# Summing k and v in four column tiles, and the gate on VectorE

## The chip, the cores and the metric

One core of a Trainium2 chip runs the kernel. The metric is the device time of one execution in microseconds, as the median of several runs. PE (TensorE) multiplies and writes PSUM, DVE (VectorE) and ACT (ScalarE) work element by element, POOL (GpSimd) does a little of that and issues some DMAs, and SP (SyncE) only issues DMAs. Each engine takes its instructions in the order in which they are written; a semaphore wait holds all that stands behind it on that engine.

## The reference

Two branches read the same x (2048 rows of 512) and are mixed row by row by a gate. Branch a is attention with 32 heads of 16 columns that share one k and one v; branch b is a dense layer with a squared relu.

```python
g = sigmoid((x * gate_w).sum(-1))
q = x @ wq            # 32 heads x 16
k, v = x @ wk, x @ wv # 16 columns each, shared by all heads
a = softmax(q k^T * 16 ** -0.5) v, heads side by side, @ wo
b = relu(x @ w1 + b1) ** 2 @ w2 + b2      # 1792 hidden columns
out = g * a + (1 - g) * b
```

All of it is in float32. The kernel forms products of large operands in pieces: each operand is rounded to a value `r` that TensorE takes at its fast rate and a rest `l`, and three products (rr, rl, lr) are added.

## The kernel before

The program is unrolled and written in the order in which the engines are to work. It has an opening, a long sequence of phases, and an end.

**The opening (lines 246 to 596).** x comes in transposed, in four chunks of 512 rows with four 128-row pieces each (`xf`, `xk`). A matrix `wkv` of 64 columns holds wk, wv, gate_w and 31 columns of zeros, so that one product gives k, v and the gate's argument. `kv_half` (L290) does it in two column tiles of 64: pieces 0 and 1 go to partitions 0 to 63 and 64 to 127 of one PSUM bank, then pieces 2 and 3 are added there. `kv_copy` (L299) brings the bank to SBUF on ScalarE. `k_rows` (L302) adds up the two halves and repeats the keys for the heads with one more product; ScalarE squares (`k_square`) and rounds them (`k_round`), `k_norm` (L315) sums the squares on TensorE and takes their maximum on VectorE, `k_parts` builds `k_aug`. The maximum over all four chunks gives a bound that `k_shift` (L324) writes into a row of `k_aug`; scores need it. `v_tiles` (L332) turns v, and the gate's argument as a seventeenth column, into rows, with one product for each 128 rows; with `idle=1` a product of 240 columns whose result nobody reads follows each. `v_rows` copies v to `v_ext` and the gate's argument to `z`. Nine of the sixteen tiles come ahead of the first phase with their idle products, seven behind it without (L1210). `q_early` makes the first q, `q_direct` and `qnorm` send it to the first score operand `qa`.

**The phases (lines 1134 to 1234).** Each phase writes scores for a few blocks (L763, into `s` banks that ScalarE turns into exponentials at L800, or into the one spare bank `x`, from which VectorE copies them at L784 first), mixes them with products of a "unit" (L1107), and ends with the context products over earlier exponentials (L814; four column tiles of 32, eight records for each 512 columns of four heads). Units are first fifteen q products, then hidden units of the dense layer (`hidden`, L651) and their sums. When a unit is through, its bank is evicted on VectorE at the end of a phase (for a q unit L392 to L396, for a hidden unit L662, L663 and `split`, L192 and L193). A second bank takes the next unit; the one after needs the evicted one.

**What orders the rest.** A planner in the Python code keeps clocks for TensorE, VectorE and ScalarE (`at_pe`, `at_dve`, `at_act`). `spend` (L621) fits small tasks on VectorE into what it takes for free time: first `soon`, with fixed due times, then `divisions`, then `chores` in their order. A chore that starts a load returns the time for which the following chores are held back (`LANDS`, 6 us, for the load of wo at L942). `soon` holds, among others, the gate (L517: two exponentials of `z` on ScalarE, four small steps on VectorE), due in the fourteenth span.

**DMAs.** Nearly all loads and the writes of q (`qs`) stand in SP's queue in written order; the low part of q goes through POOL. Ten tiles named "of" serve q's parts, norms and the hidden parts by turns.

Of the kernel before, what the change touches and what calls it, by code (L numbers as in the profile page):

```python
# [57 lines left out]

C_ID, C_BLK, C_A, C_ONE, C_SEL, C_REP, C_N = 0, 128, 160, 161, 162, 179, 307


def constants():
    c = np.zeros((128, C_N), np.float32)
    c[:, :128] = np.eye(128)
    for p in range(128):
        c[p, C_BLK + p // 32 * 2 + p % 2] = 1.0
    for r in range(2):
        c[64 * r + 16:64 * r + 32, C_A] = -1.0
    c[:, C_ONE] = 1.0
    for a in (0, 64):  # L70
        for d in range(17):
# [91 lines left out]
@with_exitstack  # L163
def mix_kernel(ctx: ExitStack, tc: tile.TileContext, xT, wkv, wq, wo, w12, b1, b2, cst, out):
    nc = tc.nc
# [62 lines left out]
    with fast, tc.tile_pool(name="at", bufs=1) as at, \  # L228
# [42 lines left out]
        wq_load(slice(1, KT))  # L271
        nc.gpsimd.dma_start(b1t, b1)

        blk = at.tile([128, 32], BF, name="blk")
# [9 lines left out]
        kvp = [sp.tile([128, 2, CH], F32, name="s") for _ in range(2)]  # L284
        ks = {0: kvp[0][:, 0], 1: kvp[0][:, 1], 3: kvp[1][:, 0]}
        sqk = at.tile([96, NC, CH], BF, name="sqk", tag="e", bufs=5)
        kvc = at.tile([128, NC, CH], F32, name="kvc", tag="e", bufs=5)
        kvq, kb = {}, {}

        def kv_half(c, a):  # L290

            if a == 0:
                kvq[c] = mp.tile([128, CH], F32, name="mm")
            for i in range(2):
                k = 2 * a + i
                nc.tensor.matmul(kvq[c][64 * i:64 * i + 64], wkvf[:, k], xf[c, k], start=a == 0, stop=a == 1,  # L296
                                 skip_group_check=True, tile_position=(0, 64 * i))

        def kv_copy(c):  # L299
            nc.scalar.activation(kvc[:, c], kvq[c], AF.Copy)  # L300
# [14 lines left out]
        def k_norm(c):  # L315
            pn = kvp[0][:, 0] if c > 1 else mp.tile([128, CH], F32, name="mm")
            nc.tensor.matmul(pn, ones, sqk[:, c], start=True, stop=True)
            return lambda: nc.vector.tensor_reduce(kmx[:, c:c + 1], pn, AX.X, OP.max)
# [13 lines left out]
        def v_tiles(tiles, vp, idle=0):  # L332

            for i in tiles:
                c, j = divmod(i, 4)
                nc.tensor.matmul(vp[:, i * 17:i * 17 + 17], kvc[:, c, j * 128:(j + 1) * 128],
                                 cs[:, C_SEL:C_SEL + 17], start=True, stop=True)
                for _ in range(idle):
                    nc.tensor.matmul(vp[:, 272:], ones, sqk[:, 0, 272:], start=True, stop=True)

        def v_rows(vp):
            vz = vp[:, :16 * 17].rearrange("p (i d) -> p i d", i=16)
            nc.vector.tensor_copy(v_ext[:, :, 0:32:2], vz[:, :, :DH])
            nc.vector.tensor_copy(z, vz[:, :, DH])

# [189 lines left out]

        qa[0] = at.tile([128, 2, CH], F32R, name="qa", bufs=2)
        kv_half(0, 0)
        x_pair(0, 0)
        kv_half(0, 1)
        kv_copy(0)  # L540
        x_pair(0, 1)
        nc.vector.tensor_copy(blk, cs[:, C_BLK:C_BLK + 32])
        qr, ql, q_round, q_rest = q_early()
        k_rows(0)
        x_pair(1, 0)
        q_round()
# [3 lines left out]
        q_direct(RS + 1, ql, DH, (nc.sync, nc.gpsimd))  # L550
        kv_half(1, 0)
        kv_half(1, 1)
        k_square(0)
        k_round(0)
        norm = k_norm(0)
        x_pair(1, 1)
        norm()
        kv_copy(1)
        kv_half(2, 0)
        kv_half(2, 1)  # L560
        k_rows(1)
        kv_copy(2)
        qnorm([(0, sq8[:, 0])], bank())
        k_square(1)
        k_round(1)
        k_parts(0)
        kv_half(3, 0)
        kv_half(3, 1)
        k_parts(1)
        kv_copy(3)  # L570
        wq_round(1)
        wq_rest(1)
        k_rows(2)
        norm = k_norm(1)
        norm()
        k_square(2)
        k_round(2)
        k_rows(3)
        norm = k_norm(2)
        norm()  # L580
        k_square(3)
        vp = ap.tile([128, CH], F32, name="acc")
        v_tiles(range(3), vp, 1)
        norm = k_norm(3)
# [6 lines left out]
        k_shift(0, True)  # L591
        v_tiles(range(3, 9), vp, 1)
        k_parts(3)
# [11 lines left out]
        soon += [(6, 1.2, lambda k=k: x_split(2, k)) for k in range(KT)]  # L605
        soon += [(10, 1.2, lambda k=k: x_split(3, k)) for k in range(KT)] + [(14, 2.0, gate)]
        ring, h, b2t, x, osp = [], [], [], dict(enumerate(zip(xr, xl))), {}

        def later(f, *args):
            chores.append((1.2, lambda: f(*args)))  # L610

        def have(half, n):
# [324 lines left out]
        def o_ready(c):  # L937

            if c == 0 and not wos:
                wos.extend(xp.tile(sh, F32R, name=n, tag=t) for n, t in (("wor", "xr2"), ("wol", "xl2")))  # L940

                def load(a):  # L942
                    nc.sync.dma_start(stage()[:, :2], wo[a * 256:a * 256 + 256].rearrange("(t p) n -> p t n", p=128))
# [75 lines left out]
        def work():  # L1019
# [3 lines left out]
            def places(unit):  # L1023
# [3 lines left out]
                def ready(p):  # L1027
                    assert not narrow
                    big = xp.tile(sh, F32, name="big", tag="xr3")
# [179 lines left out]
        evicted = True  # L1209
        v_tiles(range(9, 16), vp)  # L1210
        v_rows(vp)
# [74 lines left out]
```

## Time and profile before

| | us |
|---|---|
| median of 3 runs | 1226.75 (1225.81 to 1229.14) |
| the profiled execution | 1228.71 |
| its span | 1227.0 |
| ScalarE busy in it | 1035.5 |
| VectorE busy in it | 771.2 |

A busy TensorE at 99% says little by itself, since its matmuls overlap and their ends are modelled. What helps is a table of stretches, with TensorE's busy time and the clock that it was granted, and the timeline where one of the two is low. A step from one context group (L814) to the next serves as a yardstick, because the phases are alike: a group of 16 records closes a phase with four score blocks, a group of 24 one with six.

### The profile page before, as it was taken

Reading aid. Unit: us, or ns where it says so; the run is one execution under the profiler, and the core shown is the slowest. Engines: PE = TensorE matmul, PEld = TensorE weight load, DVE = VectorE, ACT = ScalarE, POOL = GpSimd, SP = SyncE. Lnnn points to the kernel's source line nnn. Section 1 sums busy time; section 2 is a strip of 40 time slices with the busy share of each in tenths; the row PEclk is TensorE's granted clock in tenths of the full one; section 3 lists DMA queues with packets and bytes.
Section 4 is the critical chain, followed back from the end, with each engine's and each line's share of the span. In section 5 each row is a group of like instructions: output and inputs, shape, how many; then the busy total and the mean of one; then the engine's idle time right before and its main releaser. Section 6 shows DMA issues by size and latency. Waiting matters only on the chain.

```text
span 1227.0 us, 24104 instructions
## 1 busy us (share of the span) xinstructions
PE 1211.2 (99%) x9839; PEld 673.4 (55%) x9839; DVE 771.2 (63%) x1516; ACT 1035.5 (84%) x1146; POOL 66.3 (5%) x87
## 2 busy tenths in 40 slices
PE   9999989999999999999999999999999999999997
PEld 4555545555555555555555555555555555555553
DVE  5765768466576864837678574655848476663643
ACT  6788868888988888888888888988888888988875
POOL 1001020000000200000002001000010000001000
PEclk9999989999999999999999999999999999999999
DMA  6344331121113223112133122112132222113011
GB/s 227 78 120 117 102 88 49 48 75 40 52 57 120 88 74 91 53 32 66 57 100 117 57 61 92 49 40 74 38 91 64 57 67 81 36 31 91 23 52 37
DMA packets 45347, 88.71 MB, mean 72 GB/s; under 512 B 10642, under 2 KB 10898, under 8 KB 44720
## 3 DMA queue, kind: packets, MB, share of 16 engines
q1 hardware_dynamic: 37024, 68.27, 18.7%
q0 software_dynamic: 8064, 18.59, 4.9%
q8 instruction: 79, 1.29, 0.5%
q14 instruction: 36, 0.29, 0.1%
q10 hardware_dynamic: 144, 0.26, 0.1%
HBM read 57.83 MB, written 20.97 MB: 64 GB/s over the span
## 4 chain that ended last, share of the span: by engine, by line
PE 93%; DVE 2%; ACT 2%; DMA 1%; SPq 1%; issue 1%; DVEq 0%; ACTq 0%
PE acc L814 37%; PE mm L1107 33%; PE s L763 17%; PE x L763 6%; ACT e L800 1%; DVE e L784 1%; SPq L420 1%; DMA stage<-in_wo 0%; DMA xf<-in_xT 0%; PE mm L296 0%; PE mm L200 0%; DVE qr L392 0%; DVE ql L393 0%; PE s L306 0%; DVE ot L1249 0%
## 5 line engine op out<-in xcount | busy, mean ns | idle before, releaser
L800 ACT ACTIVATE e<-s 128x1024 f32<-128x1024 f32 x822 | 781.7, 1026 | 165.9 <-PE s L763 165.3
L784 DVE COPY e<-x 128x512 f32<-128x512 f32 x404 | 279.1, 691 | 389.1 <-PE x L763 354.1
L814 PE MATMUL acc<-e,v_ext 128*32 128x512 f32 (+1 forms) x4224 | 484.3, 586 | 0.0
L763 PE MATMUL s<-qa,k_aug 49*128 49x512 f32 x1644 | 462.4, 413 | 0.2
L763 PEld LDWEIGHTS s<-qa,k_aug 49*128 49x128 f32 x1644 | 234.8, 185 | 75.0 <-ACT e L800 54.0
L814 PEld LDWEIGHTS acc<-e,v_ext 128*32 128x32 f32 x4224 | 116.1, 109 | 241.9 <-issue 238.2
L1107 PE MATMUL mm<-w2r,hr 64*128 64x512 f32 x896 | 229.2, 402 | 0.0
L800 ACT ACTIVATE e<-e 128x1024 f32<-128x1024 f32 x202 | 214.7, 1063 | 0.8 <-DVE e L784 0.8
L763 PE MATMUL x<-qa,k_aug 49*128 49x512 f32 x404 | 164.7, 408 | 5.4 <-DVE e L784 4.2
L1107 PEld LDWEIGHTS mm<-w2r,hr 64*128 64x128 f32 x896 | 135.7, 186 | 45.9 <-DVE hr L193 9.2
L1107 PE MATMUL mm<-w2l,hr 64*128 64x512 f32 x448 | 143.9, 392 | 0.0
L763 PEld LDWEIGHTS x<-qa,k_aug 49*128 49x128 f32 x404 | 75.1, 186 | 51.3 <-DVE w2l L491 12.6
L1107 PEld LDWEIGHTS mm<-w2l,hr 64*128 64x128 f32 x448 | 80.5, 186 | 6.9
L1107 PE MATMUL mm<-xragain,w1r 64*128 64x512 f32 x224 | 76.3, 418 | 0.2
L1107 PE MATMUL mm<-xr,w1r 64*128 64x512 f32 x224 | 74.3, 416 | 0.0
L1107 PE MATMUL mm<-xlagain,w1r 64*128 64x512 f32 x224 | 74.0, 391 | 0.0
L1107 PE MATMUL mm<-xragain,w1l 64*128 64x512 f32 x224 | 73.1, 392 | 0.0
L1107 PE MATMUL mm<-xl,w1r 64*128 64x512 f32 x224 | 72.4, 391 | 0.0
L1107 PE MATMUL mm<-xr,w1l 64*128 64x512 f32 x224 | 72.0, 395 | 0.0
L839 DVE RECIPROCAL n<-n 128x86 f32<-128x86 f32 x90 | 61.5, 683 | 1.8
L1107 PEld LDWEIGHTS mm<-xragain,w1r 64*128 64x128 f32 x224 | 38.2, 185 | 27.7 <-issue 9.2
L1107 PEld LDWEIGHTS mm<-xr,w1r 64*128 64x128 f32 x224 | 37.9, 185 | 26.8 <-issue 8.4
(162 smaller groups left out, 1181.4 us busy)
## 6 DMA issues: line engine op xcount, KB each, us to landing
stage<-in_w SPq DMA_DIRECT2D x56, 256.0 KB
qa<-qs SPq DMA_DIRECT2D x186, 64.0 KB
w1f<-in_w SPq DMA_DIRECT2D x28, 256.0 KB
w2f<-in_w SPq DMA_DIRECT2D x28, 256.0 KB
qs<-qr SPq DMA_DIRECT2D x16, 256.0 KB
ress<-res POOLq DMA_DIRECT2D x4, 1024.0 KB, 5.1
qs<-ql POOLq DMA_DIRECT2D x15, 256.0 KB, 7.5
oc<-accs SPq DMA_DIRECT2D x30, 128.0 KB
```

The costliest lines, as they stand in the source:

```text
L420: nc.sync.dma_start(bass.AP(tensor=o.tensor, offset=o.offset, ap=[[KS * 2 * CH, 4], [CH, 2], [1, CH]]), nrm[32 * i:32 * i + 8].bitcast(F32))
L763: nc.tensor.matmul(dst.rearrange("p (a n) -> p a n", a=2), k_aug[rows, kt * 128:(kt + 1) * 128], qa[it][rows, :, q * HC:q * HC + HC], star ...
L784: nc.vector.tensor_copy(e_half(u)[:, 2 * r:2 * r + 2], x.rearrange("p (a n) -> p a n", a=2))
L800: nc.scalar.activation(e_half(u), src, AF.Exp, scale=SCALE)
L814: nc.tensor.matmul(acc[h * 32:(h + 1) * 32, cols], v_ext[:, kt], es[u // 2][:, h % 2 * 2 + h // 2, mine], start=(kt == 0), stop=(kt == NK ...
L839: return ((0.23, bound), (0.35, compare), (0.72, lambda: nc.vector.reciprocal(n[0], n[0])), (0.28, lambda: nc.vector.tensor_tensor(o[:, co ...
L1107: nc.tensor.matmul((self.before if r else self).bank, a[p], b[p], start=not r and i == 0, stop=r == 1 and i == len(self.terms[1]) - 1, ski ...
```

## The change

- `wkv` has 32 columns (wk and wv), and `kv_sums` does the four pieces of a chunk as four column tiles of 32 at once, each in its own 32 partitions of the bank. `k_rows` and `v_tiles` add up four strips instead of two by the constant matrices. The weights' load moves from the head of SP's queue to ScalarE's. The bank is "mm" for even chunks and the spare bank "x" for odd ones.
- The gate's argument is no longer a column of that product. Sixteen blocks of 128 rows of x, not transposed, and gate_w broadcast to all partitions are loaded by SP in four groups (`gate_load`), into "of" tiles; VectorE multiplies each with gate_w and sums along the row in one instruction (`gate_sum`, L621 of the changed kernel). These are chores ahead of all others, each group held for 10 us. The gate itself is a chore behind them, and `gated` makes sure of it when the first hidden unit is evicted.
- The load of wo holds its chores back for 14 us (`WRITES`) instead of 6.
- The opening is written in another order, norms share one half of the second `s` tile, and 12 v tiles stand ahead of the first phase, 4 behind it, all with idle products.

```diff
-LANDS, DIVIDES, SURE = 6.0, 10.0, 0.7
+LANDS, DIVIDES, WRITES, SURE = 6.0, 10.0, 14.0, 0.7
...
-        wkvf = at.tile([128, KT, 64], F32, name="wkvf", tag="w1f")
-        nc.sync.dma_start(wkvf, wkv)
+        wkvf = at.tile([128, KT, 32], F32, name="wkvf", tag="w1f")
+        nc.scalar.dma_start(wkvf, wkv)
...
-            for i in range(2):
-                k = 2 * a + i
-                nc.tensor.matmul(kvq[c][64 * i:64 * i + 64], wkvf[:, k], xf[c, k], start=a == 0, stop=a == 1,
-                                 skip_group_check=True, tile_position=(0, 64 * i))
+            for k in parts:
+                nc.tensor.matmul(kvq[c][32 * k:32 * k + 32], wkvf[:, k], xf[c, k], start=True, stop=True,
+                                 skip_group_check=True, tile_position=(0, 32 * k))
...
-            pn = kvp[0][:, 0] if c > 1 else mp.tile([128, CH], F32, name="mm")
+            pn = kvp[0][:, c % 2] if c in (1, 2) else norms
...
-            nc.vector.tensor_copy(z, vz[:, :, DH])
...
-        soon += [(10, 1.2, lambda k=k: x_split(3, k)) for k in range(KT)] + [(14, 2.0, gate)]
+        soon += [(10, 1.2, lambda k=k: x_split(3, k)) for k in range(KT)]
...
+        def gate_load(i):
+            if i == 0:
+                nc.sync.dma_start(gwb, bass.AP(tensor=gw.tensor, offset=gw.offset, ap=[[0, 128], [1, D]]))
+            gates.extend(of_tile("xs", F32) for _ in range(4))
+            for j in range(i, i + 4):
+                nc.sync.dma_start(gates[j], xs[j])
+            return DIVIDES
+
+        def gate_sum(i):
+            nc.vector.scalar_tensor_tensor(gates[i], gates[i], 1.0, gwb, op0=OP.mult, op1=OP.mult,
+                                           accum_out=z[:, i:i + 1])
+
+        for i in range(NS):
+            if i % 4 == 0:
+                chores.append((0.0, lambda i=i: gate_load(i)))
+            chores.append((0.7, lambda i=i: gate_sum(i)))
+        chores.append((2.0, gate))
...
-                    return LANDS
+                    return WRITES
...
-        v_tiles(range(9, 16), vp)
+        v_tiles(range(12, 16), vp, 1)
```

Three places show how the instructions move. First TensorE in the opening, from the first sums of k and v (`mm` or `x` from `wkvf`) to the last chunk's; `cs` holds the constant matrix of `k_rows`, `ones` and `blk` are the norms' weights. Before:

```order
L296 MATMUL mm<-xf,wkvf 64x512 x4
L200 MATMUL mm<-xf,wqf 128x512 x4
L306 MATMUL s<-kvc,cs 128x512
L296 MATMUL mm<-xf,wkvf 64x512 x4
L317 LDWEIGHTS ones
L317 MATMUL mm<-sqk,ones 128x512
L296 MATMUL mm<-xk,wkvf 64x512 x4
L306 MATMUL s<-kvc,cs 128x512
L413 LDWEIGHTS blk
L413 MATMUL mm<-sq_142,blk 32x512
L296 MATMUL mm<-xk,wkvf 64x512 x4
```

Now:

```order
L297 MATMUL mm<-xf,wkvf 32x512 x4
L200 MATMUL mm<-xf,wqf 128x512 x4
L297 MATMUL x<-xf,wkvf 32x512 x4
L307 MATMUL s<-kvc,cs 128x512
L297 MATMUL mm<-xk,wkvf 32x512 x4
L307 MATMUL s<-kvc,cs 128x512
L412 LDWEIGHTS blk
L412 MATMUL s<-sq_143,blk 32x512
L318 LDWEIGHTS ones
L318 MATMUL s<-sqk,ones 128x512
L307 MATMUL mm<-kvc,cs 128x512
L297 MATMUL x<-xk,wkvf 32x512 x4
```

The second chunk's sums stand ahead of the first key rows, the first norm of the keys moved behind the q norm, and both norms are now in the same half tile.

Second, VectorE around the first two evictions of hidden units (`big` from `mm` with b1, then the square and the two parts); `wor` and `wol` are the parts of wo. Before:

```order
L784 COPY e<-x 128x2x256 x2
L662 TENSOR_SCALAR big<-mm,b1t 128x512
L663 TENSOR_TENSOR big<-big 128x512
L192 CAST hr<-big 128x512
L193 TENSOR_TENSOR hr<-big,hr 128x512
L784 COPY e<-x 128x2x256
L491 TENSOR_TENSOR w1l<-stage,w1r 128x512
L784 COPY e<-x 128x2x256
L192 CAST wor<-stage 128x512
L193 TENSOR_TENSOR wol<-stage,wor 128x512
L784 COPY e_1883<-x 128x2x256
```

Now:

```order
L806 COPY e<-x 128x2x256 x2
L519 TENSOR_SCALAR g<-g 128x16
L520 RECIPROCAL g<-g 128x16
L519 TENSOR_SCALAR omg<-omg 128x16
L520 RECIPROCAL omg<-omg 128x16
L684 TENSOR_SCALAR big<-mm,b1t 128x512
L685 TENSOR_TENSOR big<-big 128x512
L192 CAST hr<-big 128x512
L193 TENSOR_TENSOR hr<-big,hr 128x512
L806 COPY e<-x 128x2x256
L490 TENSOR_TENSOR w1l<-stage,w1r 128x512
L806 COPY e<-x 128x2x256
```

The gate, which stood 100 rows further up, is now ahead of the first eviction, and the splits of wo are gone from here: the first now follows the second hidden unit and one more w1 split.

Third, SP's queue at the same place, from the norm writes on. Before:

```order
L420 DMA qs<-nrm 4x2x512 x4
L943 DMA stage<-in_wo 128x2x512
L1033 DMA big<-in_b 128x512
L474 DMA stage<-in_w 128x512
L943 DMA stage<-in_wo 128x2x512
L474 DMA w1f<-in_w 128x512
```

Now:

```order
L419 DMA qs<-nrm 4x2x512 x4
L1056 DMA big<-in_b 128x512
L965 DMA stage<-in_wo 128x2x512
L473 DMA stage<-in_w 128x512
L473 DMA w1f<-in_w 128x512
L204 DMA oc<-accs 64x512
```

The load of b2 changes places with the first load of wo, and the second load of wo moves behind the next load of q.

More of the change, by code (lines that the diff above doesn't have):

```diff
@@ L69, in constants @@
     c[:, C_ONE] = 1.0
-    for a in (0, 64):
-        for d in range(17):
+    for a in range(0, 128, 32):
+        for d in range(DH):
             c[a + 16 + d, C_SEL + d] = 1.0
@@ L163, in mix_kernel @@
 @with_exitstack
-def mix_kernel(ctx: ExitStack, tc: tile.TileContext, xT, wkv, wq, wo, w12, b1, b2, cst, out):
+def mix_kernel(ctx: ExitStack, tc: tile.TileContext, xT, xs, gw, wkv, wq, wo, w12, b1, b2, cst, out):
     nc = tc.nc
@@ L272, in mix_kernel @@
         nc.gpsimd.dma_start(b1t, b1)
+        gwb = at.tile([128, D], F32, name="gwb", tag="lc", bufs=2)
         blk = at.tile([128, 32], BF, name="blk")
@@ L335, in v_tiles @@
                 c, j = divmod(i, 4)
[L336 to L337 removed]
+                nc.tensor.matmul(vp[:, i * DH:i * DH + DH], kvc[:, c, j * 128:(j + 1) * 128],
+                                 cs[:, C_SEL:C_SEL + DH], start=True, stop=True)
                 for _ in range(idle):
@@ L550, in mix_kernel @@
         q_direct(RS + 1, ql, DH, (nc.sync, nc.gpsimd))
-        kv_half(1, 0)
-        kv_half(1, 1)
+        kv_copy(1)
+        kv_sums(2)
         k_square(0)
         k_round(0)
[L555 to L560, printed above, removed]
+        kv_copy(2)
         k_rows(1)
-        kv_copy(2)
-        qnorm([(0, sq8[:, 0])], bank())
+        qnorm([(0, sq8[:, 0])], norms)
         k_square(1)
@@ L566, in mix_kernel @@
         k_parts(0)
-        kv_half(3, 0)
-        kv_half(3, 1)
+        norm = k_norm(0)
+        norm()
+        k_rows(2)
+        k_square(2)
+        kv_sums(3)
         k_parts(1)
         kv_copy(3)
+        norm = k_norm(1)
+        norm()
         wq_round(1)
         wq_rest(1)
[L573 to L576, printed above, removed]
+        vp = ap.tile([128, CH], F32, name="acc")
+        v_tiles(range(3), vp, 1)
+        k_rows(3)
         k_round(2)
-        k_rows(3)
         norm = k_norm(2)
@@ L581, in mix_kernel @@
         k_square(3)
-        vp = ap.tile([128, CH], F32, name="acc")
-        v_tiles(range(3), vp, 1)
+        v_tiles(range(3, 6), vp, 1)
         norm = k_norm(3)
@@ L591, in mix_kernel @@
         k_shift(0, True)
-        v_tiles(range(3, 9), vp, 1)
+        v_tiles(range(6, 12), vp, 1)
         k_parts(3)
```

32 lines of the change are left out of this document (20 added, 12 removed).

## The prediction

> **What bounds the kernel now.** First a row of the page (busy time of the engines), then the stretches of ten microseconds (columns: length, then busy time of PE, PEld, DVE, ACT, POOL, then the granted clock, the DMA share and GB/s).
>
> ```profile
> PE 1211.2 (99%) x9839; PEld 673.4 (55%) x9839; DVE 771.2 (63%) x1516; ACT 1035.5 (84%) x1146; POOL 66.3 (5%) x87
> ...
> 20.00:30.00 10.00, 9.87 (x62) 7.08 (x60) 8.70 (x18) 8.36 (x13) 0.67 (x2) 1.00 0.34 99
> 30.00:40.00 10.00, 9.85 (x70) 6.31 (x69) 7.32 (x16) 6.76 (x8) 0.66 (x1) 0.83 0.35 106
> ...
> 160.00:170.00 10.00, 6.87 (x55) 3.65 (x51) 3.47 (x7) 5.77 (x7) 0.59 (x1) 0.94 0.51 155
> 170.00:180.00 10.00, 9.63 (x59) 3.71 (x59) 7.20 (x12) 5.37 (x6) 6.35 (x4) 0.72 0.21 54
> ```
>
> TensorE is busy 99% of the span, so the change cannot win by sparing VectorE or ScalarE as such. It wins where TensorE stands still or runs at a lower clock, and these rows show two such places: 30 to 40, and 160 to 180, where TensorE is idle for 3.1 us of ten and the clock then falls to 0.72. The change touches both, besides the opening. The profiled execution took 1228.71 us (span 1227.0), 1.96 us over the median 1226.75. I make the sum against the former and subtract it from the median, since neither place belongs to profiling alone, as far as one execution can tell.
>
> **Term 1, the stall at 163 us: -6.4 us.** The timeline of all engines (start, length, engine, and in brackets the idle time before and its releaser):
>
> ```profile
> 162.96 1.92 PE L814 MATMUL acc<-e,v_ext 128*32 128x512 f32 x16
> 163.31 0.45 SPq L943 DMA_DIRECT2D stage<-in_wo  x1
> ...
> 168.56 0.43 DVE L192 CAST wor<-stage 128x512 fp32r<-128x512 f32 x1 [5.34 <-DMA stage<-in_wo]
> ...
> 170.37 0.79 PE L763 MATMUL x<-qa,k_aug 49*128 49x512 f32 x1 [3.44 <-DVE e L784]
> ...
> 171.95 3.64 PE L814 MATMUL acc<-e,v_ext 128*32 128x512 f32 x16
> ...
> 178.12 1.92 PE L814 MATMUL acc<-e,v_ext 128*32 128x512 f32 x16
> ```
>
> VectorE reaches the first cast of wo before its load, which SP issued late, has landed. The score copy queued behind the cast waits, TensorE waits for the copy (3.44 us), the clock halves, and the contexts show it (3.64 us for what takes 1.92). Undisturbed contexts of 16 products are 4.38 us apart:
>
> ```profile
> 101.47 2.78 PE L814 MATMUL acc<-e,v_ext 128*32 128x512 f32 x24
> 106.75 1.92 PE L814 MATMUL acc<-e,v_ext 128*32 128x512 f32 x16
> 111.13 1.92 PE L814 MATMUL acc<-e,v_ext 128*32 128x512 f32 x16
> ```
>
> From 162.96 to 178.12 are 15.16 us for two steps of 4.38: 6.4 us too many. The changed order of VectorE has the first cast of wo behind the next hidden unit, and the wait built into the planner grows from 6 to 14 us. There it is behind the copies and w1 splits that follow the context now at 178.12, so with the stall gone its turn comes after 172, and nearer to 175. SP issues the load behind the same norm writes as now and behind the load of b2, near 163.8, and it lands near 169 (5.25 us from 163.31 to 168.56, as now). The cover is 3 to 6 us; if it goes, the stall is back, and up to whole. The second load stands behind the next q load on SP, and its splits stand far behind it, among the first sums into res.
>
> **Term 2, the gate leaves its old place: -0.6 us.**
>
> ```profile
> 68.26 2.78 PE L814 MATMUL acc<-e,v_ext 128*32 128x512 f32 x24
> 68.85 0.17 DVE L520 TENSOR_SCALAR g<-g 128x16 f32<-128x16 f32 x1 [3.52 <-ACT g L519]
> 69.38 0.25 DVE L521 RECIPROCAL omg<-omg 128x16 f32<-128x16 f32 x1
> 71.54 0.50 PE L1107 MATMUL mm<-xr,wqr 64*128 64x512 f32 x2 [0.51 <-DVE ql L393]
> ...
> 74.11 1.92 PE L814 MATMUL acc<-e,v_ext 128*32 128x512 f32 x16
> ```
>
> VectorE waits 3.52 us for ScalarE's exponential, which is queued behind score exponentials. The context step here is 74.11 - 68.26 = 5.85, against 106.75 - 101.47 = 5.28 undisturbed: 0.57.
>
> **Term 3, the gate at its new place: +1.35 us.** It stands right ahead of the first hidden unit's eviction:
>
> ```profile
> 157.38 2.78 PE L814 MATMUL acc<-e,v_ext 128*32 128x512 f32 x24
> 157.43 0.74 DVE L662 TENSOR_SCALAR big<-mm,b1t 128x512 f32<-128x512 f32 x1
> ...
> 158.44 1.06 ACT L800 ACTIVATE e<-e 128x1024 f32<-128x1024 f32 x1
> 159.38 0.63 ACT L496 ACTIVATE w1r<-stage 128x512 fp32r<-128x512 f32 x1
> ...
> 160.09 0.50 PE L1107 MATMUL mm<-xr,w1r 64*128 64x512 f32 x2
> ```
>
> The exponential follows the last score exponential, where w1r stands now (159.38). I give it 0.25 until VectorE has it, and VectorE's four steps 0.78, as now (68.85 to 69.38 + 0.25). The eviction then starts at about 160.4 instead of 157.43 and reads its bank until 161.1. The next unit's products need that bank: they start at 161.15 instead of 160.09, 1.06 late. The score copy behind the four eviction steps then holds the second score in the spare bank, some 0.5 more, of which 0.2 to 0.3 is already in the present step (162.96 - 157.38 = 5.58). In all 1.35; between 0.5, if ScalarE is early, and 2.
>
> **Term 4, the sums on VectorE: +0.2 us.** Sixteen products with a running sum over 128x512. The trace has none. The nearest rows of the grouped view (count, then busy, mean ns, idle before), and two of the gaps in the timeline of VectorE:
>
> ```profile
> L321 DVE SCALAR_TENSOR_TENSOR k_aug<-kb,cs,s 128x512 fp32r<-128x512 f32 x3 | 2.1, 736 | 0.0
> L836 DVE DVE_READ_ACCUMULATOR lc<-n,lc 128x1 f32 x90 | 7.5, 83 | 0.0
> ...
> 109.14 0.69 DVE L784 COPY e<-x 128x512 f32<-128x512 f32 x1 [1.82 <-PE x L763]
> 149.47 0.69 DVE L784 COPY e<-x 128x512 f32<-128x512 f32 x1 [2.32 <-PE x L763]
> ```
>
> I take 0.7 + 0.08 each, 12.5 us in all. Nine stand alone ahead of a score copy that waits 0.8 us or more for TensorE; three each stand together ahead of the copies at 109.14 and 149.47, 2.3 us into gaps of 1.82 and 2.32: half a microsecond over at the first. Against that, one takes the place of a longer split near 46 us, where VectorE sets TensorE's pace, for some 0.3. From -0.5 (the splits spread out help more) to +2 (each sum takes twice its row). The loads, 4 MB more, are bounded below as a rival.
>
> **Term 5, the opening: -0.7 us.** Rows of the opening:
>
> ```profile
> 6.77 1.08 PE L296 MATMUL mm<-xf,wkvf 128*64 128x512 f32 x4 [0.28 <-DMA xf<-in_xT]
> 7.78 3.70 PE L200 MATMUL mm<-xf,wqf 128*128 128x512 f32 x8
> 12.27 1.94 PE L296 MATMUL mm<-xf,wkvf 128*64 128x512 f32 x8
> 23.26 1.14 ACT L512 ACTIVATE wqr<-wqf 128x512 fp32r<-128x512 f32 x2
> 23.71 0.69 DVE L318 TENSOR_REDUCE kmx<-s 128x1 f32<-128x512 f32 x1 [0.48 <-PE s L317]
> 24.82 0.62 ACT L328 ACTIVATE k_aug<-km 1x512 fp32r<-1x512 f32 x1 [0.42 <-DVE km L590]
> ```
>
> Two column tiles take 1.94 us a chunk (four pairs of 0.43 and a tail). Four at once take 2 x 0.43 + 0.2 = 1.08, as four context products do (24 records, six groups, 2.78 us). So TensorE is spared 0.86 us on three chunks, 2.6 us; the first chunk waits for its halves as before. Moving one load off SP's front brings x about 0.4 us earlier. But TensorE does not set the end here. I follow the new order with these durations. The q product ends at 11.1 (11.48 now), the second chunk's sums at 12.0, the first key rows at 12.8 (0.86 and a tail each). ScalarE squares and rounds them until 13.9 (0.57 a step); only then may the second key rows be written, until 15.0, and they are rounded at 16.1. VectorE builds keys, a maximum, keys (0.7 each) until 18.4, which frees the bank for the second norm. That product, three v tiles, the last key rows, their square and the last norm (0.2, 0.85, 1.05, 0.65, 0.7) bring the last maximum to 21.9, its end to 22.6, against 24.4 now. Now ScalarE's rounding of the last keys waits for that maximum, since both read one PSUM tile, and two wq roundings and the shift row stand behind it: 22.6 + 0.6 + 0.6 + 0.5 + 0.6 = 24.8 against 25.44. First scores 0.7 us earlier; with the maximum anywhere between 21.6 and 23.3, 1.7 to 0.
>
> [...]
>
> **Term 6, the clock at 32 us: -1.45 us.**
>
> ```profile
> 29.82 1.74 PE L336 MATMUL acc<-cs,kvc 128*128 128x17 f32 x14
> ...
> 32.00:32.50 0.50, 0.35 (x3) 0.14 (x2) 0.50 (x3) 0.22 (x1) 0.00 (x0) 0.73 0.00 0
> ...
> 35.50:36.00 0.50, 0.50 (x6) 0.44 (x4) 0.36 (x1) 0.00 (x0) 0.00 (x0) 0.86 0.57 180
> ```
>
> The seven v products of 17 columns are hardly work for the array, and behind them the clock is at half for 3.4 us, in which TensorE had full rows to do: 3.4/2 = 1.7, less 0.25 that ScalarE would hold back. The change leaves four here, each followed by a product of 240 columns, the mixture that the six tiles ahead of phase 0 ran in with the clock at 1.00 (the row of 20 to 30 above). I expect the fall to go; if not, 0.
>
> [...]
>
> **The sum.** -6.4 - 0.57 + 1.35 + 0.2 - 0.7 - 1.45 = -7.5: 1228.7 to 1221.2 in a profile, 1226.75 to **1219.2** in the median. Behind 250 us all engines' rows stand as before.
>
> **The rivals.**
> - The clock falls all the same, at 32 or at 25, where TensorE will now wait about a microsecond for the shift row: -6.0, **1220.7**. For it: the new wait; against it: the padding.
> - The change does not do what it says in the opening: four f32 tiles run two by two, or x lands no earlier. Each chunk is 0.86 late, the opening gains nothing and may lose 1: **1220 to 1221**. Against it: the context rows.
> - The stall comes back once, at the moved wo split or at one group of sums, whose loads stand in SP's queue among writes: +6.4, **1225.6**. Also here: the stall of 163 us was larger under the profiler than without it.
> - Slower: the loads of x for the sums land after the sums' turn at two or more of the four places. Each then costs what wo's wait cost, 6.4; two make -7.5 + 12.8, **1232**. It decides when a load is later than its slack. The closest is the second group, whose last load waits for the write of the third q unit's low part; these rows show it (issue, median landing, the copy ahead of the first sum):
>
> ```profile
> 59.14 0.69 POOL L355 DMA_DIRECT2D qs<-ql  x1 [8.31 <-issue]
> ...
> qs<-ql POOLq DMA_DIRECT2D x15, 256.0 KB, 7.5
> ...
> 81.12 0.69 DVE L784 COPY e<-x 128x512 f32<-128x512 f32 x1 [0.35 <-PE x L763]
> ```
>
> 59.1 + 7.5 + 5.25 as wo took is 71.9; the first sum's turn is at 81.8. Ten microseconds in hand speak against it.
>
> **How the numbers follow.** The forecast has 0.42, the clock 0.2, the opening 0.1, the stall once 0.2, slower 0.08. A measurement of this kernel tells 0.3%, 3.7 us, from no change. Faster by that (under 1223.1) are the first three, 0.72; within it is the fourth, 0.2; slower the last, 0.08. The range goes down to 1216 (opening -1.7, gate at +0.5, VectorE at -0.5 add up to 2.6, and half a microsecond for the rest) and up to 1226, which takes in the stall once and, on the forecast, the gate at 2 and VectorE at 2; it leaves out the slower case.
>
> **What would show it.** Right: no DVE wait for the load of wo, contexts 4.4 us apart from 163 to 180, a clock of 1.00 from 30 to 40, a wait of about 2 us of VectorE for ScalarE's g ahead of the first hidden eviction, k and v products of 8 records in 1.1 us, first context near 35.4. Wrong: a DVE wait for xs or wo of microseconds, or contexts from 40 to 150 further apart than now.

## The result, and the profile after

The changed kernel takes **1232.55 us** (median of 7 runs, 1231.12 to 1237.21), the kernel before 1226.38 us on the same chip (7 runs): a ratio of 1.0049, 95% interval 1.0029 to 1.0069. It is slower by 6 us, where the forecast was 7.5 us faster, and lies outside the range. The profiled execution took 1232.21 us (span 1230.4).

First the stretches of ten microseconds of the changed kernel, with the columns of the prediction (length, then busy time of PE, PEld, DVE, ACT, POOL, then granted clock, DMA share, GB/s):

```profile
20.00:30.00 10.00, 9.05 (x56) 7.16 (x57) 7.90 (x16) 6.85 (x11) 0.00 (x0) 0.87 0.66 208
30.00:40.00 10.00, 10.00 (x58) 6.93 (x61) 5.67 (x12) 7.34 (x8) 0.00 (x0) 0.62 0.40 125
110.00:120.00 10.00, 6.78 (x48) 4.08 (x46) 4.39 (x8) 5.01 (x7) 0.69 (x1) 0.81 0.61 169
120.00:130.00 10.00, 9.81 (x70) 4.25 (x70) 5.73 (x10) 6.86 (x8) 0.70 (x1) 0.85 0.40 104
160.00:170.00 10.00, 9.13 (x77) 5.41 (x73) 5.81 (x13) 7.69 (x11) 0.70 (x1) 1.00 0.36 70
170.00:180.00 10.00, 9.51 (x75) 4.77 (x75) 6.88 (x10) 8.41 (x9) 5.31 (x4) 1.00 0.38 122
```

The hole at 160 to 180 is closed: TensorE is busy for 9.13 and 9.51 us and its clock stays whole. But a hole of the same depth stands at 110 to 130, and the clock between 30 and 40, which was to rise from 0.83 to 1.00, has fallen to 0.62. The contexts, set side by side in order, show where the time went (start before, start after, and what each stretch added):

| up to the context at | after | late by | added in the stretch | forecast |
|---|---|---|---|---|
| 37.52 (the first) | 38.96 | 1.44 | +1.44 | -2.15 (terms 5 and 6) |
| 74.11 | 74.78 | 0.67 | -0.77 | -0.57 (term 2) |
| 126.96 | 133.65 | 6.69 | +6.02 | +0.2 (term 4) |
| 162.96 | 170.91 | 7.95 | +1.26 | +1.35 (term 3) |
| 178.12 | 180.50 | 2.38 | -5.57 | -6.4 (term 1) |
| 1213.78 (the last) | 1216.13 | 2.35 | -0.03 | 0 |
| end of the span, 1227.0 | 1230.4 | 3.4 | +1.05 | 0 |

Three rows are near the forecast, two are far off, and the last had no forecast. (The table gives 3.4 of the 6.2 us between the medians; the rest is that the profiled execution of before took 2.3 us more than its median and that of after 0.3 less.) The first of the two, around 113 us, in the timeline (start, length, engine, and in brackets the idle time before and its releaser):

```profile
107.91 0.70 POOL L354 DMA_DIRECT2D qs<-ql  x1 [6.93 <-DVE w2l L490]
...
111.81 1.92 PE L836 MATMUL acc<-e,v_ext 128*32 128x512 f32 x16
112.10 0.68 DVE L391 CAST qr<-mm 128x512 fp32r<-128x512 f32 x1
...
116.21 0.69 DVE L392 TENSOR_TENSOR ql<-mm,qr 128x512 fp32r<-128x512 f32 x1 [3.44 <-DMA qs<-ql]
116.41 1.77 SPq L617 DMA_DIRECT2D xs<-in_xs  x4
...
116.96 0.80 PE L1130 MATMUL mm<-xr,wqr 64*128 64x512 f32 x2 [3.22 <-DVE ql L392]
117.31 0.69 POOL L354 DMA_DIRECT2D qs<-ql  x1 [8.70 <-DVE ql L392]
```

VectorE has rounded a q unit (L391) and then stands still for 3.44 us: the buffer for the rest `ql` is not free. Its releaser is the write of the `ql` of the unit **before**, which POOL issued at 107.91, and such a write takes 7.9 us by its median on the page (107.91 + 7.9 = 115.8):

```profile
qs<-ql POOLq DMA_DIRECT2D x15, 256.0 KB, 7.9
```

TensorE waits behind VectorE for 3.22 us, and then runs at half clock (granted clock 0.50 from 116.2 to 123.0 us), as it did at 170 us in the kernel before (0.50 from 168.8 to 175.6). Why the buffer is late shows in the program's order and in the addresses of its tiles. The fourth group of four x tiles (L617, the row of SP) was given its buffers just ahead of this unit. The four tiles lie in the buffers that had been free longest, and `qr` and `ql` were left those of the unit before. In the kernel before, a unit's tiles lie in buffers that were written out two units earlier or more.

The second place is the opening. The row of keys that the first scores need, in the timeline after:

```profile
22.29 0.69 DVE L319 TENSOR_REDUCE kmx<-s 128x1 f32<-128x512 f32 x1 [0.26 <-PE s L318]
...
23.02 0.60 ACT L314 ACTIVATE kb<-s 128x512 fp32r<-128x512 f32 x1 [1.30 <-DVE kmx L319]
23.51 1.14 ACT L511 ACTIVATE wqr<-wqf 128x512 fp32r<-128x512 f32 x2
24.68 0.62 ACT L329 ACTIVATE k_aug<-km 1x512 fp32r<-1x512 f32 x1
25.35 0.51 PE L785 MATMUL s<-qa,k_aug 49*128 49x512 f32 x2 [0.95 <-ACT k_aug L329]
```

The order of ScalarE is the forecast one (keys, two roundings of wq, row), the last maximum ends at 22.98 instead of 22.6, and the first scores into `s` start 0.5 us earlier than before (25.35 against 25.88). TensorE stands still for 0.95 us ahead of them. In tenths of a microsecond the clock is at half from 27.45 to 37.7, for 10.2 us, where the kernel before has it from 32.25 to 35.65, for 3.4.

### The profile page after: what moved, and what is told of

It reads as the page before. It is cut to its first block, busy times and chain, and to the rows that moved or that the text cites. A ratio compares the mean times of both kernels' runs of the same rounds, so it can differ in the third digit from the quotient of the medians.

```text
span 1230.4 us, 24165 instructions
## 1 busy us (share of the span) xinstructions
PE 1211.8 (98%) x9845; PEld 675.8 (55%) x9846; DVE 781.4 (64%) x1547; ACT 1036.8 (84%) x1146; POOL 65.1 (5%) x87
## 4 chain that ended last, share of the span: by engine, by line
PE 88%; issue 7%; DVE 2%; ACT 1%; DMA 1%; POOL 1%; POOLq 0%; DVEq 0%; ACTq 0%
PE acc L836 34%; PE mm L1130 30%; PE s L785 16%; PE x L785 5%; ACT e L822 1%; DMA qs<-ql 1%; POOL qs L354 0%; DVE e L806 0%; PE acc L524 0%; PE mm L200 0%; DVE big L685 0%; DVE hr L193 0%; PE s L307 0%; DVE big L684 0%; PE mm L297 0%
```

## The experiments

A profile is one execution, and executions of one kernel differ by some microseconds, and in their granted clock: of 31 runs of the kernel before on one chip the fastest took 1223.27 us at a mean granted clock of 0.999 over the span, the slowest 1232.56 at 0.990. So the verdicts below go by medians of runs taken in turn with the kernel before, and the profiles tell what a run lost where.

**The stall at 163 us by itself.** The kernel before, with only the wait after the load of wo changed:

```diff
                 def load(a):
                     nc.sync.dma_start(stage()[:, :2], wo[...])
-                    return LANDS
+                    return 14.0
```

> The kernel before with one change: the wait that the planner keeps after a load of wo grows from 6 to 14 us, so VectorE's first cast of wo stands behind the next hidden unit. Theory (the stall at 163 us is this load, and worth what the trace of before shows): no wait of VectorE for stage<-in_wo, contexts 4.4 us apart from 163 to 180, 5.6 to 6.4 us less in the profile, median near 1220.5. Rival (the stall is larger under the profiler, since the profiled execution of before is 2.3 us above its median): the trace improves as much, the median by only 3.5 to 4.5, 1222 to 1223.

Measured: 1221.95 us, the kernel before 1226.26; ratio 0.9960 (0.9947 to 0.9974), so 4.9 us, 3.2 to 6.5. The rival is nearer by the medians (4.3), the interval holds both. In its trace the steps after 163 us lose 6.2 us (its contexts are late by 3.62 us at 162.96 and early by 2.54 at 178.12), and TensorE is busy throughout:

```profile
160.00:170.00 10.00, 9.94 (x84) 4.80 (x82) 5.83 (x9) 8.24 (x10) 0.00 (x0) 1.00 0.56 134
170.00:180.00 10.00, 10.00 (x86) 5.11 (x85) 7.95 (x13) 8.70 (x10) 6.29 (x4) 1.00 0.17 59
```

This part of the change works alone. The 3.62 us are the opening of the **unchanged** order: in this one execution its clock fell to 0.50 at 25.4, in the seven others the mean clock is 0.997 or more.

**First attempt on the ring, and the opening on top.** Three kernels on the changed one. `last2` takes the last four x tiles two and two; `row_first` is `last2` with ScalarE's order in the opening turned; `old_open` is `last2` with the whole opening of the kernel before.

```diff
 last2:     -            gates.extend(of_tile("xs", F32) for _ in range(4))
            +            n = 4 if i < 12 else 2
            +            gates.extend(of_tile("xs", F32) for _ in range(n))
            ...          (a load at i == 14 besides, of n tiles each)
 row_first:  k_round(3)
            -for t in (2, 3):
            -    wq_round(t)
             nc.vector.tensor_reduce(km, kmx, AX.X, OP.max)
             nc.vector.tensor_scalar(km..., 0.5, ROOT, ...)
             k_shift(0, True)
            +for t in (2, 3):
            +    wq_round(t)
```

> The changed kernel, but the last four tiles of x for the gate sums are taken two and two instead of four at once; the same sums, the same loads, the same bytes. Theory (the changed kernel waits at 112.8 us because the group of four takes the older buffers of the ring of ten just ahead of a q unit, and the unit's low part is left with the buffer of the low part before, whose write has 3.4 us to go): the wait of VectorE for qs<-ql at 112.8 goes, with the half clock behind it: 6.7 us less in the profile, median 1225 to 1227. Rival (the writes are late since the loads of x crowd the queues, whichever buffer is taken): a wait for a write of q of 2 us or more stays here or shows at another unit, median 1229 or more.

> As last2, and in the opening ScalarE writes the shift row ahead of the two roundings of wq instead of behind them. Theory (TensorE's wait of 0.95 us for this row, from 24.40 to 25.35, is what lets the clock fall at 27.4 for 10.4 us): first scores into s at 24.3 instead of 25.35, clock at 1.00 until at least 30, the first context 2 to 3.5 us earlier than in last2, median 1222 to 1224. Rival (the clock falls for another reason, the thin products of the opening as a whole): first scores 1 us earlier, but the half clock stays near 27 and as long; 0 to 1 us less than last2.

> As last2, but with the opening of the kernel before (k and v of a chunk summed in two column tiles, its order, its v tiles of 17 columns, the load of its weights first on SP); the gate's sums on VectorE stay. Theory (the new opening is a loss of 1.4 us at the first context, by the longer half clock): first context near 37.5, clock at half from 32 to 35.5 alone, median 1.4 us under last2, 1224 to 1225. Rival (the new opening wins 0.5 us or more as it does at the first scores, and the loss at 39 us is made up later where TensorE waits anyway): median the same as last2 or up to 0.7 above.

Measured: `last2` 1231.28, `row_first` 1226.55, `old_open` 1228.10, before 1226.26 (ratios 1.0027, 0.9986 and 1.0009, each give or take 0.0019 or less). All three miss their forecasts (`row_first` 1222 to 1224, `old_open` 1224 to 1225), and the stall that follows is in all three. In `last2` the wait at 112.8 us is gone, but the last pair is now loaded at 158 us, right ahead of the gate, and VectorE waits for it:

```profile
158.13 0.82 SPq L618 DMA_DIRECT2D xs<-in_xs  x2
...
161.21 0.69 DVE L622 SCALAR_TENSOR_TENSOR xs<-xs,gwb 128x512 f32<-128x512 f32 x1 [1.78 <-DMA xs<-in_xs]
```

So it moved the stall instead of removing it, and says nothing on the ring's price. `row_first` is 4.7 us under `last2`, more than the microsecond of the scores: its clock is whole from 20 to 45 us, and its first context stands at 34.74 instead of 40.20. `old_open` has its first context at 37.16 and its half clock from 31.8 to 35.3 alone, as forecast. Its median is 3.2 under that of `last2`, but the intervals of the two ratios overlap, and in the traces its stall at the gate is 3.5 us shorter, so these two don't price the new opening.

**Pairs throughout, and is it the idle time?** `pairs6` takes all x tiles two at a time and lets the sums follow 6 us after a load; `pairs6_row` adds the turned order; `pairs6_pad` leaves the order and adds six idle products ahead of the first scores instead; `no_sums` leaves out loads and sums.

```diff
 pairs6:     -for _ in range(4)        pairs6_pad: -v_tiles(range(6, 12), vp, 1)
             +for _ in range(2)                    +v_tiles(range(6, 12), vp, 2)
             -return DIVIDES           no_sums:    -gate_load(i), gate_sum(i) as chores
             +return LANDS                         +nc.vector.memset(z, 0.0)
             ... (a load at every second i)
```

> The changed kernel, but all tiles of x for the gate sums are taken two at a time, and a pair's sums may follow 6 us after its load instead of 10, so the last pair comes some 40 us before the gate. Theory (what the changed kernel loses between 110 and 170 us are waits that the tiles of x make: the crowded ring at 112.8, or in the version with the last four two and two a load that comes too late): no wait of VectorE over 1 us for qs<-ql or xs<-in_xs, contexts from 75 to 160 as far apart as before, median 1226 to 1227, 5 to 6 us under the changed kernel. Rival (sums and loads cost as such, wherever the buffers are): over 1229.

> As pairs6, and ScalarE writes the shift row ahead of the two roundings of wq. Theory (TensorE's wait of about a microsecond ahead of the first scores makes the clock fall longer in the opening, which took 4.7 us off the median of the version before): 4 to 5 us under pairs6, near 1222, and the mean granted clocks of its runs 0.997 or more. Rival (that difference was chance): within 1.5 us of pairs6.

> As pairs6, and each of the six v tiles ahead of the first scores is followed by two products of 240 columns instead of one, so that TensorE has work for 0.7 us of the 0.95 that it waits for the shift row; ScalarE's order stays. If it is TensorE's idle time that makes the clock fall: most of what the moved row gives, 3 to 4 us under pairs6, with the first scores at the same time as there. If the moved row helps by its time alone (scores a microsecond earlier), or the products do not count as work: within 1 us of pairs6.

> The changed kernel without the loads of x for the gate and without the sixteen sums (z is set to zero, so the gate is one half everywhere; the gate's six small steps go back to about 68 us by themselves). Left of the change: the opening and the longer wait after the load of wo. Theory (opening a loss by its longer half clock, about 3 us in the median; wo 4.3 won): 1225 to 1226, with mean clocks of 0.990 to 0.995 as in the changed kernel. Rival (the opening wins as forecast, and all of the loss is in the gate): 1220 to 1221.5.

Measured: `pairs6` 1236.84, `pairs6_row` 1232.13, `pairs6_pad` 1232.66, `no_sums` 1224.09, before 1227.16 (ratios 1.0076, 1.0049 to 1.0102; 1.0034, 1.0017 to 1.0051; 1.0039, 1.0024 to 1.0055; 0.9975, 0.9960 to 0.9990). `pairs6` is a miss on the other side: 6 us are too few for the loads, and the waits for them cost more than the ring did. The view of the waits of `pairs6` (us in total, times, longest):

```profile
DVE xs L621 <- DMA xs<-in_xs: 9.9, 4, 5.1
```

This is the slower rival of the prediction, made by the experiment; the changed kernel, with its 10 us, has no such wait. For the clock in the opening the three are clear. Between 22 and 40 us the granted clock (after POOL's column) is, for `pairs6`, for `pairs6_pad` and for `pairs6_row`:

```profile
22.00:40.00 18.00, 17.05 (x86) 13.11 (x86) 11.09 (x24) 12.02 (x15) 0.00 (x0) 0.62 0.48 154
```

```profile
22.00:40.00 18.00, 16.99 (x119) 11.40 (x118) 13.91 (x28) 12.61 (x15) 0.90 (x1) 0.91 0.51 159
```

```profile
22.00:40.00 18.00, 17.47 (x132) 10.96 (x134) 15.71 (x32) 13.77 (x17) 0.89 (x1) 1.00 0.58 181
```

and their rows of the first scores into `s`:

```profile
25.32 0.51 PE L785 MATMUL s<-qa,k_aug 49*128 49x512 f32 x2 [0.95 <-DMA gwb<-in_gw]
```

```profile
24.97 0.73 PE L785 MATMUL s<-qa,k_aug 49*128 49x512 f32 x3 [0.34 <-ACT k_aug L329]
```

```profile
23.93 0.78 PE L785 MATMUL s<-qa,k_aug 49*128 49x512 f32 x3
```

(The first names the load of the gate's weights; the row of keys ends at 25.27 there, 0.05 us earlier, and that the scores wait for.) The first context stands at 40.48, 36.72 and 34.63. Products that nobody reads, put in the place of idle time, bring it 3.8 us forward, though the scores come only 0.35 us earlier: in these three profiles the early fall of the clock (0.62, against 0.91 and 1.00) goes with TensorE's idle time ahead of the scores (0.95 us, against 0.34 and none), and the time of the scores alone doesn't tell it: `only_gw`, further down, starts them at 24.98, as `pairs6_pad` does at 24.97, but behind 0.95 us of idle time, and has 0.72. The medians are 4.2 (products) and 4.7 us (turned order) lower, but they don't price the opening. In the profiled executions the waits for x between 106 and 120 us take up most of what the opening gave, and the last contexts stand at 1217.53, 1217.32 and 1216.31. And the clocks of `pairs6_row`, forecast at 0.997 or more, are 0.993 to 0.998.

`no_sums` shows the new opening and the mended wo alone, with the gate back at 68 us: 3.1 us under the kernel before, against 4.3 to 4.9 for wo alone. The intervals overlap, so the loss by the new opening is not shown by the times; by the clock it is, with a mean of 0.993 to 0.996 in all twelve runs of `no_sums` and 0.997 or more in seven of the eight of `wait14`. By the ratios `no_sums` is 0.74%, 9.1 us, under the changed kernel, which is what sums, loads and the gate's new place cost there.

**The ring relieved, and the parts put together.** `stage2` leaves groups, waits and bytes as they are in the changed kernel, and puts two of four tiles elsewhere, from the second group on. `stage2_row` adds the turned order, `gate_early` also issues ScalarE's two exponentials of the gate when the last sum is issued. `wait14_pad` is `wait14` with idle products behind the seven bare v products.

```diff
 stage2:     -gates.extend(of_tile("xs", F32) for _ in range(4))
             +gates.extend(of_tile("xs", F32) if i == 0 or j > 1 else stage()[:, j] for j in range(4))
 gate_early: -chores.append((2.0, gate))
             +chores.append((0.0, ...both exponentials...)); VectorE's steps run in gated()
 wait14_pad: -v_tiles(range(9, 16), vp)
             +v_tiles(range(9, 16), vp, 1)
```

> The changed kernel, but two of the four tiles of x in the second, third and fourth group lie in the first half of the stage buffer, which nothing uses between 31 and 163 us, so the ring of ten gives up two buffers instead of four. Groups of four, the wait of 10 us after a load, sums and bytes are those of the changed kernel. Theory (what the sums cost there is the crowded ring: a q unit left with the buffer of the unit before it): no wait of VectorE for qs<-ql at 112.8, contexts from 110 to 160 as far apart as before, 6 to 7 us under the changed kernel, 1226. Rival (loads and sums cost it anyway, as in the version with pairs 6 us after their loads, where VectorE waited 9.9 us for xs): waits of VectorE for xs<-in_xs of over 2 us, 1230 or more.

> As stage2, with the shift row ahead of the two roundings of wq. If both causes add up: 4 to 5 us under stage2, 1221 to 1222, no half clock ahead of 30 us. If the half clock only moves to a later place once the early one is gone: under 2 us below stage2.

> As stage2_row, and ScalarE's two exponentials of the gate are issued when the last sum is, so only VectorE's four short steps are left ahead of the first hidden eviction. Theory (the gate's new place costs 1.25 us, most of it the wait for the exponentials): 0.7 to 1.2 us under stage2_row. Rival (ScalarE now waits for the last sum with score exponentials behind it): the same or up to 1 us over stage2_row.

> The kernel before with the longer wait after the load of wo, and with each of the last seven v products followed by a product of 240 columns. Theory of the prediction (the seven bare products of 17 columns make the clock fall at 32 us, the padding keeps it): no half clock from 32 to 35.5, 1 to 1.5 us less than with the longer wait alone, 1220.5 to 1221. Rival (padding costs TensorE 0.8 us and the clock falls all the same, or the fall comes from elsewhere): 0 to 1 us more, 1222 to 1223.

Measured, before 1228.49 on this chip: `stage2` 1226.86 (ratio 0.9996, 0.9983 to 1.0008), `stage2_row` 1221.75 (0.9958, 0.9945 to 0.9971), `gate_early` 1220.03 (0.9941, 0.9921 to 0.9961), `wait14_pad` 1221.91 (0.9960, 0.9945 to 0.9975). `stage2` at the unit that waited in the changed kernel:

```profile
112.11 0.68 DVE L391 CAST qr<-mm 128x512 fp32r<-128x512 f32 x1
112.83 0.69 DVE L392 TENSOR_TENSOR ql<-mm,qr 128x512 fp32r<-128x512 f32 x1
```

No wait, and 0.53% (1.0049 to 0.9996; with both intervals 0.3 to 0.76%), 6.5 us, are gone, as the ring was priced. It also prices the sums by themselves: against the kernel before, its contexts are late by 0.69 to 0.73 us at every start from 74.11 to 157.38, so the twelve sums in that stretch, and the loads beside them, cost the contexts nothing in this execution.

`stage2_row` gives 5.1 us more: the causes add up. `gate_early` gives 1.7 more, a little over the theory, but the intervals of the two ratios overlap. In its trace the stretch up to the context at 162.96 loses nothing (0.30 us less than before, as in `no_sums`), where that of `stage2_row` has +1.25. Its VectorE takes the gate's steps without a wait, where the changed kernel has one of 2.11 us:

```profile
158.34 0.17 DVE L518 TENSOR_SCALAR g<-g 128x16 f32<-128x16 f32 x1
```

```profile
166.33 0.17 DVE L519 TENSOR_SCALAR g<-g 128x16 f32<-128x16 f32 x1 [2.11 <-ACT g L518]
```

`gate_early` has the lowest median of this study, 0.59% under the kernel before (0.39 to 0.79%), and the four ideas of the change are all in it. (Its profiled execution took 1224.13 us, 4.1 above the median; VectorE waits 4.44 us for a load of w1 there, at 84.68.) But the wait after the load of wo gives 0.40% by itself (`wait14`, 0.26 to 0.53%), and these intervals overlap: that the other three add to it is not shown.

`wait14_pad` has no half clock between 20 and 45 us, and ten of its twelve runs have a mean clock of 0.999 or more, against 0.997 to 0.998 in six of eight of `wait14`. But its ratio is that of `wait14` (0.9960 both): with the padding the clock holds at 32 us there, as the prediction had it, and no gain in time is seen, though the intervals would hide one of 1 to 1.5 us. Nor is the padding always enough. The four v tiles of the changed kernel are padded too, and of the five kernels with that opening and a whole clock up to 31 us, four keep it (`row_first`, `pairs6_row`, `stage2_row`, `gate_early`). In `pairs6_pad` it falls at 31.7 us for 3.4, right behind another gap:

```profile
31.48 0.59 PE L1130 MATMUL mm<-xr,wqr 64*128 64x512 f32 x1 [0.67 <-DVE peek L1231]
```

**The microsecond at the end.** From the start of the last context to the end of the span are 13.0 to 13.4 us in the four kernels without loads for the gate (before, `wait14`, `wait14_pad`, `no_sums`), and 13.9 to 14.3 in the ten others so far, which have them, though the last write is issued 8.3 us behind that context in both (1213.78 to 1222.12 before, 1216.13 to 1224.46 after). Two kernels put back one half of the loads each, without sums:

```diff
 only_gw:  +chores.append((0.0, only_gw))            # gwb <- gw, read by nothing
 only_xs:  +chores.append((0.0, lambda i=i: gate_load(i)))   # for i in 0, 4, 8, 12; no gwb
```

> As no_sums (no loads of x for the gate, no sums, z zero, so the gate is one half everywhere), with the one load that copies the gate's weights to all 128 partitions put back, at 21 us; nothing reads it. It asks for the microsecond behind the last context: from its start to the end of the span are 13.0 to 13.4 us in the four kernels without loads for the gate and 13.9 to 14.3 in the ten with them. If this load makes it (its descriptors, its place in the program): 13.9 or more. If the loads of x make it: 13.0 to 13.4. Median as no_sums, within 1 us.

> As no_sums, with the sixteen loads of x for the gate put back in their groups of four, but no sums and no load of the gate's weights; z is zero. If the loads of x make the last microsecond: 13.9 us or more from the last context to the end, else 13.0 to 13.4. If the loads alone, without VectorE's sums, crowd the ring: a wait of VectorE for qs<-ql of over 2 us and 4 to 7 us over no_sums; if a tile that no sum holds comes free at once: no such wait, within 1 us of no_sums.

Measured: 1224.98 and 1223.88 us, before 1226.54 (ratios 0.9980, 0.9966 to 0.9995, and 0.9983, 0.9964 to 1.0001), and 13.72 and 13.42 us at the end. Neither bound is met by the first, and the second is at the edge: inconclusive. That microsecond stays unexplained. In `only_xs` sixteen loads without sums cost nothing clear of noise against `no_sums`, and no unit waits for its buffer. But with no sums between them its groups are issued at 22, 40, 51 and 64 us, where the changed kernel has 22, 64, 96 and 116, so no group stands ahead of the unit that waited there. That a tile which no sum holds comes free at once fits this, and isn't shown by it.

## Why the prediction was wrong, point by point

Two steps failed: term 4, which put nothing at the ring of buffers, by 6 us, and terms 5 and 6, whose clock in the opening went the other way, by 3.6.

**Term 1 (wo, -6.4): right in kind, a little too large.** -5.57 in the trace after, -6.2 in that of `wait14`, and 3.2 to 6.5 in the runs. The last case of the prediction's third rival, that the stall is larger under the profiler, may hold a part of it; the interval doesn't settle it.

**Term 2 (the gate's old place, -0.57): right.** From the context at 61.10 to that at 74.11 the changed kernel gains 0.58 (late by 1.25, then by 0.67).

**Term 3 (the gate's new place, +1.35): right.** +1.26 in the trace. When the wait for ScalarE is taken out (`gate_early`), 1.55 go in the trace and 1.7 by the medians, the latter not clear of noise.

**Term 4 (the sums, +0.2): this step failed, by 6 us.** The price of the sums themselves was right: 0.68 + 0.08 us each, and nothing on the path. What the step left out is where their tiles lie. It counted the loads of x as what could be late, and found ten microseconds in hand; but the tiles come out of the ring of ten that the q units use, each of which needs two buffers whose last contents have left by a write of 7.9 us. Four x tiles taken at once, ahead of a unit, leave it the buffers of the unit before, whose write has 3.4 us to go. The wait then costs 3.44 us on VectorE, 3.22 on TensorE, and nearly as much again (6.02 in all) by the half clock. `stage2` is the proof: the same sums, groups, waits and bytes, and the 6.5 us are gone. That alone would not have saved the forecast: `stage2` is level with the kernel before, not faster. The rival that came to 1232 had the right time by luck, since its mechanism was another (loads behind the sums' turn), and `pairs6` shows that mechanism as a different one, with its own row.

**Term 5 (the opening, -0.7): the chain was right, its consequence was missed.** Scores 0.5 us earlier, and the four column tiles take 1.06 us a chunk, as the contexts had promised. But the chain ends on ScalarE, and the spared TensorE time became a gap of 0.95 us ahead of the first scores.

**Term 6 (the clock at 32 us, -1.45): this step failed too.** The clock does hold there with the padding in `wait14_pad` (no half clock between 20 and 45 us), though with no gain in time that can be seen, but in the changed kernel the clock falls earlier, behind that gap, and for three times as long (10.24 us against 3.41). The first rival named the place and the wait ("at 25, where TensorE will now wait about a microsecond for the shift row"); it priced it as the gain that is lost and not as a longer fall. Terms 5 and 6 came to +1.44 instead of -2.15 in the trace. The order of ScalarE that makes the gap, with its microsecond of later scores and the half clock behind it, costs 4.7 and 5.1 us by the medians (`last2` and `row_first`, `stage2` and `stage2_row`), and 5.0 and 4.6 at the last contexts of their traces.

**The end (+1.05) was in no term**, and is open.

Set together, in ratios to the kernel before: wo -0.40%, ring +0.53%, the opening, the gate and the end the rest of the +0.49%, +0.36%. Mended at three places, the same change is 0.59% faster than before, of which wo's 0.40% is the part that is shown by itself.

## What to carry to other kernels

When tiles are added to a ring that others use, ask not only whether the new loads come in time, but which buffer the old users are left with, and set the age of its last write against that write's landing time. When work is taken off TensorE, look for the gap that it leaves: here a half clock of ten microseconds (10.24 in the changed kernel) stood behind 0.95 us of idle time. Filling it with products that nobody reads brought the first context 3.8 us forward, and turning the order of two steps on another engine 4.4 to 5.9. And where runs of one kernel spread by more than the effect, change one part at a time against the same chip, since one profile's opening may be luck: that of `wait14`, with the order of before, has the latest first context of all (41.14 us), in a kernel that is faster than before.

## What the runs showed of the hardware

In windows of a tenth of a microsecond, the granted clock of the opening is 0.50 for 3.41 us in the kernel before (from 32.23) and for 10.24 in the changed kernel (from 27.46); at the stalls it is 0.50 for 6.83 us in each (from 168.76 before, from 116.17 after). The two longer lengths are 2.00 and 3.00 times the shortest; what sets them is not shown. From 22 to 40 us the mean clock is 0.91 in the kernel before and in `pairs6_pad`, 0.72 in the changed kernel, `only_gw` and `only_xs`, and 0.62 in `pairs6`.

All seven profiles of this opening with the gap of 0.95 us ahead of the first scores have an early fall. In `after` it comes 2.1 us behind the start of those scores (27.46 against 25.35), in `stage2` 1.3 (26.71, 25.38), in `only_gw` 1.2 (26.13, 24.98), in `only_xs` 1.0 (26.30, 25.33), in `last2` with them (25.04) and in `no_sums` 0.1 ahead of them (25.27, 25.41); `pairs6` has the mean of 0.62. In the one profile with 0.34 us there (`pairs6_pad`) the clock stayed until 31.7 us, and in the four with the turned order and no gap at that place (`row_first`, `pairs6_row`, `stage2_row`, `gate_early`) it stayed throughout; its mean from 22 to 40 us is 1.00 in `pairs6_row` and `stage2_row`. In the order of before, which has no such gap, it came early in one of four profiles (`wait14`, at 25.4, against before, `old_open` and `wait14_pad`), so not every early fall had a gap ahead of it, and what made it fall there is open.
